# Attention and mixer block on one core: another order of operations, and twenty small operations on another engine

## The chip, the cores and the metric

The kernel runs on one core of one Trainium2 chip. The metric is the device time of one execution in microseconds (us); three executions of the kernel before gave 193.62, 194.53 and 194.60, so the median is 194.53. The five engines of a core are called PE (matmul), ACT (ScalarE), DVE (VectorE), POOL (GpSimd) and SP (SyncE, which here only issues transfers). Each runs its own instructions in order and waits for the others by semaphores.

## What is computed

x has 2048 rows of 448 numbers in bf16. Part A is an attention over 16 heads of 28 numbers in which each row sees 8 rows, itself and every second one before it; part B is a mixer that shifts quarters of the columns by one or two rows, followed by an MLP of width 1792.

```python
def _A_ref(x, wqkv, wo):
    W, dil = 8, 2
    ...
    logits = jnp.einsum("bhsd,bhswd->bhsw", q, kg) * scale
    attn = _softmax(logits, axis=-1)
    o = jnp.einsum("bhsw,bhswd->bhsd", attn, vg)
    return (...)(o, 0, 2, 1, 3).reshape(B, S, D) @ wo

def _B_ref(x, w1, w2, w3, w4):
    h = _gelu(_layernorm(x, axis=-1) @ w1)
    ...
    hs = jnp.concatenate([g0, g1, g2, g3], axis=-1) @ w2
    x1 = x + hs
    h2 = _gelu(_layernorm(x1, axis=-1) @ w3) @ w4
    return x1 + h2

h = x + _A_ref(_layernorm(x, axis=-1), A_wqkv, A_wo)
h2 = h + _B_ref(_layernorm(h, axis=-1), B_w1, B_w2, B_w3, B_w4)
```

## The kernel before

**Tiling and stages.** The 2048 rows are 16 tiles of 128, in four blocks t = 0 to 3 of 512 rows. All weights and x lie in SBUF once loaded. Part A runs for each block through N1 (layernorm, line 663), A1 (queries and keys, 679), V (values, 720), A2 (741) and A3 (788); part B through B1 (834), B2 (873), W3 (911) and B3 (928). The stages of part B behind B1 use other groups of tiles, the units u = 0 to 4 with tiles 0-1, 2-5, 6-9, 10-13 and 14-15.

The names that the prediction uses, each with its block or unit as a digit:
- A2: VectorE multiplies queries with shifted keys into `qk_r` (128 x 4096, three times a block, and once 128 x 2048), PE sums over `zc`. S: softmax on VectorE and ScalarE; its last product, into `pb`, is on VectorE or, by a table, on GpSimd; PE transposes `pb` and the result is copied out of PSUM.
- A3: VectorE spreads the weights over a mask into `bd_r`, PE multiplies by `vw` (the values, shifted by transfers from `vt` into `vw`; a few such transfers a block), and the results are copied into `actT`. O: the output projection with `wo_s`, added to x in `xin`.
- B1: layernorm of block t (its last step, the norms, writes `lntm`); a DMA transpose of 128 x 2048 numbers turns `lntm` into `actT`; M: PE multiplies by w1 (`w_s` in the profile's names), ScalarE applies gelu and writes into `arena`.
- B2: PE multiplies by w2 (`ps<-w_s,arena`), VectorE adds into `arena`; T: layernorm of unit u and its DMA transpose into `actT` (half as wide for units 0 and 4). W3: PE multiplies by w3, ScalarE's gelu writes `h3T`. B3: PE multiplies `h3T` by w4, VectorE adds and writes `ost`, which SyncE stores.

M0, W30, T0 and so on are these stages for block or unit 0. Where a sum of PE is made of two halves of 64 partitions, two groups run in pairs (`duo`).

**What sets the order.** The phases are recorded as 891 numbered operations, and one table, `ORDER` (lines 19 to 50), is a permutation of these numbers. `arrange` (192) goes through it: the operations of each engine are issued in the order of the table, each waiting by semaphores only for what it reads, overwrites or needs a buffer of. A second table, `OTHER` (51 to 53), names operations that take their alternative engine: a copy out of PSUM (`copy`, 397) or a norm (`normalize`, 552) goes to VectorE instead of ScalarE, and the product into `pb` (776) to GpSimd instead of VectorE. All instructions are issued at line 994, except the loads of ScalarE's table for exponentials and logarithms (989), so lines do not tell the groups of the profile apart; their tile names do.

All transfers go out on SyncE's queue, in the order of the table. For DMA transposes one rule is added: a transpose waits until the one before it and all plain transfers between the two have landed, and a plain transfer waits until the transposes before it have landed. Stores of results (their channel is callable) are exempt.

```python
if op.insts[0][0] == "dma_start_transpose":
    op.deps.update(turned + moved)
    turned, moved = [op], []
elif op.is_dma and not callable(op.chan):
    op.deps.update(turned)
    moved.append(op)
```

w1 and w2 are loaded by eleven transfers, w3 and w4 by two halves each (896 and 784 KB; `arena<-in_B_w_dram` in the profile).

Of the kernel before, what the change touches and what calls it, by code (L numbers as in the profile page):

```python
# [16 lines left out]
POWER = {'N1': 'aaaa', 'B1': 'aaaa', 'B2': 'apapp'}  # L17
RESIDUAL = 'ttvv'
ORDER = """
# [30 lines left out]
"""  # L50
OTHER = """
104 127 196 197 199 402 408 411 519 525 528 582 583
"""
FULL = (4,)
FILL = (1, 1, 0, 0)
# [980 lines left out]
```

## Time and profile before

| what | value |
|---|---|
| median of three executions | 194.53 us |
| span of the profiled execution, first to last instruction | 192.0 us |
| DMA traffic | 17.04 MB, 89 GB/s over the span |
| chain that ended last | PE 67%, DMA 13%, ACT 12%, DVE 3%, SyncE's queue 2% |
| DMA transposes | 9, of 4.4 us (median from issue to landing) |

The profiled execution's own time is its span; the executions that were timed lie some 2.5 us above it. Rows of the profile read: start in us, duration in us, engine, line, operation, tile written <- tiles read, shape and type, xcount for several merged, and in brackets the idle time of the engine ahead of it with what ended it. "PE ... 64*128 64x512" is a matmul of 64 rows of weights by 128 columns with 512 columns of data. `SPq` is SyncE's queue; its rows last as long as the issuing, not the transfer. Rows of a table by stages begin with the stretch from:to and then give the busy time of the engines.

### The profile page before, as it was taken

The page shows a single profiled execution, that of the slowest core. Times are in us where ns is not written, and L with a number is a line of the kernel's source. Part 1 is how long each engine was busy: PE and PEld are TensorE (multiplying, and loading weights), DVE is VectorE, ACT ScalarE, POOL GpSimd, SP SyncE. Part 2 cuts the span into 40 slices and gives each one's busy share as a digit, 9 for nine tenths or more (in the row PEclk, how much of TensorE's full clock was granted, in tenths as well). Part 3 has the DMA queues.
Part 4 walks back from the last instruction along what each step waited for, and adds up shares of the span by engine and source line. Part 5 has one row for each costly group of instructions (what it writes and reads, how often), then busy time and mean ns, then how long its engine had stood idle before and what let it go on. Part 6 is the DMA issues. An engine that isn't in the chain of part 4 may idle for free.

```text
span 192.0 us, 5741 instructions
## 1 busy us (share of the span) xinstructions
PE 181.2 (94%) x2482; PEld 92.6 (48%) x2482; DVE 129.6 (67%) x229; ACT 133.0 (69%) x310; POOL 29.3 (15%) x63
## 2 busy tenths in 40 slices
PE   6999999999999869969999999999999999999994
PEld 2584533453444333337545444455444544555672
DVE  7899999999999999999876970036988022002203
ACT  4489999999999999998595898860158004731340
POOL 3240000000004000201067000022077700000000
DMA  5998792005504163935905014006200542000111
GB/s 146 353 282 175 194 295 44 14 0 133 133 3 90 23 66 72 319 64 125 113 3 106 8 34 103 0 0 126 58 26 1 109 106 73 0 3 0 51 48 48
DMA packets 30273, 17.04 MB, mean 89 GB/s; under 512 B 18936, under 2 KB 29736, under 8 KB 30248
## 3 DMA queue, kind: packets, MB, share of 16 engines
q1 hardware_dynamic: 30248, 16.68, 37.1%
q8 instruction: 19, 0.31, 0.7%
q14 instruction: 6, 0.05, 0.1%
HBM read 8.04 MB, written 1.84 MB: 51 GB/s over the span
## 4 chain that ended last, share of the span: by engine, by line
PE 67%; DMA 13%; ACT 12%; DVE 3%; SPq 2%; issue 1%; POOL 0%; POOLq 0%; ACTq 0%
PE ps L994 67%; DMA actT<-lntm 7%; DMA arena<-in_B_w_dram 3%; ACT lntm L994 3%; ACT arena L994 3%; DMA vw<-vt 2%; ACT vt L994 2%; SPq L994 2%; DVE bd_r L994 2%; ACT h3T L994 1%; ACT actT L994 1%; ACT xin L994 1%; DVE lntm L994 1%; DVE ost L994 1%; ACT ls L994 1%
## 5 line engine op out<-in xcount | busy, mean ns | idle before, releaser
L994 PE MATMUL ps<-actT,arena 64*128 64x256 bf16 (+1 forms) x756 | 68.7, 329 | 2.2 <-DMA actT<-lntm 1.7
L994 ACT ACTIVATE h3T<-ps 128x512 bf16<-128x512 f32 (+1 forms) x70 | 30.3, 525 | 40.1 <-PE ps L994 40.0
L994 PEld LDWEIGHTS ps<-actT,arena 64*128 64x128 bf16 x756 | 35.4, 94 | 31.6 <-DMA actT<-lntm 2.1
L994 PE MATMUL ps<-arena,h3T 64*128 64x448 bf16 (+2 forms) x434 | 44.4, 343 | 0.0
L994 ACT ACTIVATE arena<-ps 128x512 bf16<-128x512 f32 (+10 forms) x86 | 40.1, 515 | 3.3 <-PE ps L994 2.5
L994 DVE SCALAR_TENSOR_TENSOR ost<-ps,mrs,arena 128x448 bf16<-128x448 f32 (+1 forms) x17 | 10.7, 652 | 36.5 <-PE ps L994 36.5
L994 DVE TENSOR_TENSOR qk_r<-arena 128x4096 bf16<-128x4096 bf16 (+1 forms) x16 | 32.0, 2016 | 0.4 <-ACT arena L994 0.2
L994 PEld LDWEIGHTS ps<-arena,h3T 64*128 64x128 bf16 (+1 forms) x434 | 23.0, 94 | 18.7 <-issue 0.2
L994 POOL TENSOR_TENSOR arena<-arena,xin 128x448 f32<-128x448 f32 x16 | 17.2, 1088 | 45.0 <-DVE lntm L994 45.0
L994 DVE TENSOR_TENSOR bd_r<-arena,bmask 80x2048 bf16<-80x2048 bf16 x16 | 19.0, 1216 | 1.6 <-PE ps L994 0.9
L994 ACT ACTIVATE actT<-ps 128x512 bf16<-128x512 f32 (+2 forms) x21 | 14.6, 742 | 2.1 <-PE ps L994 2.1
L994 PE MATMUL ps<-actT,w_s 64*128 64x512 bf16 x112 | 13.3, 377 | 1.7 <-DMA actT<-lntm 1.2
L994 PE MATMUL ps<-wo_s,actT 64*128 64x448 bf16 x128 | 14.3, 350 | 0.1
L994 PE MATMUL ps<-arena,actT 64*128 64x448 bf16 x112 | 12.4, 350 | 0.4 <-ACT vt L994 0.4
L994 PE MATMUL ps<-w_s,arena 64*128 64x448 bf16 x112 | 11.6, 350 | 1.0 <-ACT arena L994 0.9
L994 ACT ACTIVATE lntm<-xin,nm 128x448 bf16<-128x448 bf16 x16 | 10.5, 660 | 2.6 <-DVE nm L994 2.6
L994 DVE SCALAR_TENSOR_TENSOR arena<-xin,rs_y,ps 128x448 f32<-128x448 bf16 x16 | 10.3, 672 | 2.2 <-PE ps L994 2.2
L994 DVE TENSOR_SCALAR lntm<-arena,mv,rs_y 128x512 bf16<-128x512 f32 x14 | 10.2, 773 | 2.1 <-POOL rs_y L994 2.0
L994 POOL TENSOR_TENSOR pb<-ls,mx 128x512 bf16<-128x512 f32 x2 | 3.3, 1641 | 52.8 <-ACT mx L994 52.8
L994 DVE BATCH_NORM_STATS2 st<-xin 128x6 f32<-128x448 bf16 x16 | 9.4, 614 | 0.8 <-DMA xin<-in_A_x_dram 0.7
L994 PEld LDWEIGHTS ps<-actT,w_s 64*128 64x128 bf16 x112 | 5.1, 94 | 8.9 <-PE ps L994 1.7
L994 PEld LDWEIGHTS ps<-wo_s,actT 64*128 64x128 bf16 x128 | 5.6, 94 | 6.7 <-PE ps L994 1.4
(73 smaller groups left out, 161.7 us busy)
## 6 DMA issues: line engine op xcount, KB each, us to landing
arena<-in_B_w_dram SPq DMA_DIRECT2D x2, 896.0 KB, 7.3
out_dram<-ost SPq DMA_DIRECT2D x15, 112.0 KB, 1.9
arena<-in_B_w_dram SPq DMA_DIRECT2D x2, 784.0 KB, 5.7
vw<-vt SPq DMA_DIRECT2D x4, 320.0 KB, 4.3
vw<-vt SPq DMA_DIRECT2D x4, 256.0 KB, 4.2
arena<-in_A_wqkv_dram SPq DMA_DIRECT2D x2, 448.0 KB, 4.6
xin<-in_A_x_dram SPq DMA_DIRECT2D x2, 448.0 KB, 7.5
xin<-in_A_x_dram SPq DMA_DIRECT2D x3, 224.0 KB, 5.6
```

The source lines that it names most:

```text
L994: inst = getattr(eng, meth)(**kw)
```

## The change

The table `ORDER` is written anew, so that the operations of every engine are issued in another order, and `OTHER` names other operations. Nothing else differs: the same 891 operations, tiles and buffers. Of `OTHER`'s entries, thirteen operations go from ScalarE to VectorE (98, 106, 414, 417 and 534, copies into `actT`; 129, 134, 253 and 365, copies of keys and their edges; 256, into `vt`; 404 and 522, softmax results; 198, a norm of block 0), seven from VectorE to ScalarE (104, 127, 408, 411, 525, 528; 196, another norm of block 0), and one, 161, the product into `pb` of S0, from VectorE to GpSimd. ScalarE so has 266 operations instead of 272, VectorE 224 instead of 219, GpSimd 60 instead of 59. ScalarE's instructions whose first partition differs from that of the one before are 50 instead of 36.

```diff
 ORDER = """
-43 8 7 2 11 0 1 49 44 45 6 9 10 12 5 39 13 40 42 58 59 60 61 63 64 62 70 68 50 51 52 53 54 55 56 57 14 65 66 71 69 67
...
+43 0 1 7 39 2 40 41 8 58 59 60 11 9 63 5 64 61 62 10 68 65 66 70 69 71 67 72 73 74 75 78 46 44 49 50 51 52 53 54 55 56
...
 """
 OTHER = """
-104 127 196 197 199 402 408 411 519 525 528 582 583
+98 106 129 134 161 197 198 199 253 256 365 402 404 414 417 519 522 534 582 583
 """
```

SyncE's queue before, first from w2's last pieces through w3's two halves, then from block 0's transpose on (DMA_TRANSPOSE of 128x16x128 are those of blocks 0 to 3 and units 1 to 3, of 128x8x128 those of units 0 and 4; the pieces of w4 are 128x7x448):

```order
L994 DMA w2_s<-in_B_w2_dram 48x448
L994 DMA w2_s<-in_B_w2_dram 64x448 x2
L994 DMA vw<-vt 64x4x512
L994 DMA arena<-in_B_w3_dram 128x2x1792
L994 DMA vw<-vt 16x3x512
L994 DMA arena<-in_B_w3_dram 128x2x1792
L994 DMA vw<-vt 16x512
```

```order
L994 DMA_TRANSPOSE actT<-lntm 128x16x128 x2
L994 DMA vw<-vt 16x3x512
L994 DMA arena<-in_B_w4_dram 128x7x448
L994 DMA vw<-vt 16x512
L994 DMA arena<-in_B_w4_dram 128x7x448
L994 DMA_TRANSPOSE actT<-lntm 128x8x128
L994 DMA vw<-vt 80x4x512
L994 DMA vw<-vt 64x4x512
L994 DMA_TRANSPOSE actT<-lntm 128x16x128 x3
```

And the same part of the queue now, where w2's last pieces and w3 come behind the copies of block 2 into `vw`:

```order
L994 DMA w2_s<-in_B_w2_dram 64x448 x2
L994 DMA arena<-in_B_w3_dram 128x2x1792
L994 DMA_TRANSPOSE actT<-lntm 128x16x128
L994 DMA arena<-in_B_w3_dram 128x2x1792
L994 DMA_TRANSPOSE actT<-lntm 128x16x128
L994 DMA_TRANSPOSE actT<-lntm 128x8x128
L994 DMA arena<-in_B_w4_dram 128x7x448
L994 DMA vw<-vt 64x4x512
L994 DMA vw<-vt 16x3x512
L994 DMA arena<-in_B_w4_dram 128x7x448
L994 DMA vw<-vt 80x4x512
L994 DMA_TRANSPOSE actT<-lntm 128x16x128
```

Unit 0's transpose has moved ahead of w4, right behind that of block 1, and w3's second half stands between the transposes of blocks 0 and 1. The loads of w1 and w2, which stood ahead of all copies into `vw`, now stand among those of blocks 1 and 2: w1 behind the first copy of block 2 and w2 behind two more.

PE before, from M1 (by w1) through block 1's part of B2 (by w2) and W30 (`ps<-actT,arena` of 256 columns) to B30:

```order
L994 MATMUL ps<-actT,w1_s 128x512 x28
L994 MATMUL ps<-qk_r,zc 32x32x8x2 x8
L994 MATMUL ps<-wo_s,actT 128x448 x8
L994 MATMUL ps<-qk_r,zc 32x32x8x2 x8
L994 MATMUL ps<-wo_s,actT 128x448 x8
L994 MATMUL ps<-qk_r,zc 32x32x8x2 x4
L994 MATMUL ps<-w2_s,arena 128x448 x28
L994 MATMUL ps<-actT,arena 128x256 x56
L994 MATMUL ps<-ident,pb 80x64 x16
L994 MATMUL ps<-actT,arena 128x256 x42
L994 MATMUL ps<-arena,h3T 128x448 x28
L994 MATMUL ps<-bd_r,vw 32x64 x96
```

PE now, from the output projections of block 2 ahead of M1 on:

```order
L994 MATMUL ps<-wo_s,actT 128x448 x24
L994 MATMUL ps<-actT,w1_s 128x512 x14
L994 MATMUL ps<-wo_s,actT 128x448 x8
L994 MATMUL ps<-actT,w1_s 128x512 x8
L994 MATMUL ps<-qk_r,zc 32x32x8x2 x8
L994 MATMUL ps<-actT,w1_s 128x512 x6
L994 MATMUL ps<-actT,arena 128x256 x42
L994 MATMUL ps<-qk_r,zc 32x32x8x2 x12
L994 MATMUL ps<-w2_s,arena 128x448 x14
L994 MATMUL ps<-actT,arena 128x256 x8
L994 MATMUL ps<-w2_s,arena 128x448 x8
L994 MATMUL ps<-actT,arena 128x256 x6
```

W30 has moved ahead of the 28 matmuls by w2, with part of which it now alternates, and 24 instead of 16 projection matmuls stand between M0 and M1.

VectorE before, around unit 0's norms (`lntm<-arena,nm,rs_y`):

```order
L994 TENSOR_TENSOR qk_r<-arena 128x4096
L994 CAST actT<-ps 128x512
L994 TENSOR_TENSOR nmr<-nm,rs_y 128x2
L994 SCALAR_TENSOR_TENSOR xin,mv<-ps,xin 128x448 x2
L994 TENSOR_TENSOR qk_r<-arena 128x2048
L994 TENSOR_SCALAR lntm<-arena,nm,rs_y 128x512 x2
L994 SCALAR_TENSOR_TENSOR xin,mv<-ps,xin 128x448 x2
```

And now:

```order
L994 TENSOR_TENSOR qk_r<-arena 128x4096
L994 TENSOR_TENSOR nmr<-nm,rs_y 128x2
L994 TENSOR_SCALAR lntm<-arena,nm,rs_y 128x512 x2
L994 SCALAR_TENSOR_TENSOR xin,mv<-ps,xin 128x448 x4
L994 TENSOR_SCALAR nm<-mv 128x4
L994 TENSOR_TENSOR qk_r<-arena 128x4096
L994 TENSOR_TENSOR qk_r<-arena 128x2048
```

The four sums into `xin`, the `qk_r` product of half width and one of full width now stand behind the norms.

58 rows, old and new, of the table ORDER are left out of this document.

## The prediction

> **What bounds the kernel now.** I read the page's busy shares first, then the busy time by stages (engines in us of each stretch), then TensorE's rows in time where a stage is not full, and last the chain of waits over those places.
>
> ```profile
> PE 181.2 (94%) x2482; PEld 92.6 (48%) x2482; DVE 129.6 (67%) x229; ACT 133.0 (69%) x310; POOL 29.3 (15%) x63
> 50.00:60.00 10.00, 9.91 (x220) 4.61 (x218) 9.94 (x15) 9.97 (x28) 0.01 (x1) 1.00 0.10 29
> 60.00:70.00 10.00, 7.56 (x174) 3.54 (x170) 9.79 (x18) 9.79 (x21) 2.19 (x1) 1.00 0.28 54
> 70.00:80.00 10.00, 9.40 (x120) 3.67 (x122) 9.84 (x17) 9.78 (x22) 0.03 (x1) 1.00 0.83 169
> 80.00:90.00 10.00, 7.98 (x118) 4.58 (x112) 9.44 (x24) 9.15 (x25) 2.53 (x4) 1.00 0.55 141
> 90.00:100.00 10.00, 9.57 (x226) 5.62 (x226) 7.47 (x11) 7.84 (x18) 2.23 (x4) 1.00 0.46 56
> 100.00:140.00 40.00, 40.00 (x402) 19.31 (x400) 22.05 (x54) 25.07 (x48) 7.19 (x8) 1.00 0.25 52
> ```
>
> The columns after the stretch are PE, PEld, DVE, ACT, POOL, the granted clock (1.00 everywhere), the DMA share and GB/s. PE is 94% busy, yet what can be won is all in one place: from 60 to 100 us PE lacks 2.44 + 0.60 + 2.02 + 0.43 = 5.49 us, and in the same stretch until 90 us VectorE and ScalarE are 92 to 98% busy. From 100 us on PE is full (40.00 of 40.00). So the end is the start of the last gap-free run of PE, plus the work behind it.
>
> ```profile
> 63.60 3.67 PE L994 MATMUL ps<-actT,w_s 64*128 64x512 bf16 x28 [0.77 <-DMA actT<-lntm]
> 74.18 3.43 PE L994 MATMUL ps<-actT,w_s 64*128 64x512 bf16 x28 [0.33 <-ACT rs_x L994]
> 85.71 3.47 PE L994 MATMUL ps<-actT,arena 64*128 64x256 bf16 x56 [1.66 <-DMA actT<-lntm]
> 96.07 1.25 PE L994 MATMUL ps<-actT,w_s 64*128 64x512 bf16 x10 [0.43 <-DMA actT<-lntm]
> ```
>
> These are M0, M1, W30 and M2: each begins when a DMA transpose has landed. The chain of waits tells why those land so late:
>
> ```profile
> 68.82 5.27 DMA actT<-lntm
> 76.09 6.49 DMA arena<-in_B_w_dram
> 82.60 3.06 DMA actT<-lntm
> 85.71 2.49 PE ps L994 x42
> 90.60 5.43 DMA actT<-lntm
> 96.07 92.72 PE ps L994 x981
> ```
>
> It is a row of transfers on SyncE's queue: block 1's transpose, w4's second half, T0's transpose, and at last block 2's transpose (90.60), with which the gap-free run of 92.72 us begins.
>
> **T0's transpose no longer waits for w4.** A transpose waits for all plain transfers queued since the one before (the rule of `arrange`), so T0's was issued at 82.60, when w4's second half had landed at 76.09 + 6.49 = 82.58, though its rows were ready earlier:
>
> ```profile
> 79.35 1.00 DVE L994 TENSOR_SCALAR lntm<-arena,nm,rs_y 128x512 bf16<-128x512 f32 x2
> 76.91 0.62 DVE L994 SCALAR_TENSOR_TENSOR xin<-ps,xin 128x448 bf16<-128x448 f32 x1
> 78.21 1.23 DVE L994 TENSOR_TENSOR qk_r<-arena 128x2048 bf16<-128x2048 bf16 x1
> 69.85 2.28 DVE L994 TENSOR_TENSOR qk_r<-arena 128x4096 bf16<-128x4096 bf16 x1
> ```
>
> The norms ended at 80.35, so 2.25 us were lost to w4. The new VectorE order also puts these norms ahead of two sums into xin (0.55 each by their starts), a half qk_r product (1.1) and a whole one (2.2), 4.4 us; of the operations that VectorE takes over (below) some 1.5 us stand ahead. That leaves 2.9 less, so they end near 77.5. With 3.06 of transfer the rows land at 80.6 instead of 85.67. PE gets there from M1's start (74.2 to 75.8, below) by 3.43, eight wo and eight zc matmuls (0.76 and 0.45 by starts), so at 78.9 to 80.5: W30's wait shrinks from 1.66 to between 0 and 1.7, five us earlier. Late next is VectorE.
>
> **Block 2's transpose then hangs on its norms alone.** Before, it was issued at 90.60, when copies queued behind T0's transpose had landed; its norms were done at 89.76 (89.38 + 0.38):
>
> ```profile
> 89.38 0.38 DVE L994 TENSOR_SCALAR lntm<-xin,nm,rs_y 128x512 bf16<-128x512 bf16 x1
> 85.68 1.38 SPq L994 DMA_DIRECT2D vw<-vt  x2
> ```
>
> The copies now follow a transpose that lands 5 us earlier; of w4's two halves among them the second goes out some 2 us behind that landing (three issues of 0.69, half of 1.38) and lands 6.49 later, at 89.1, just ahead of the norms. VectorE's work up to those norms is nearly that of before: what went behind T0's norms still stands ahead of these, two statistics of mixer rows and what goes with them (1.2 us) now stand behind, and the 1.5 us of added operations come on top: +0.3. VectorE lacks 0.56 us in 80 to 90 and was full before that, so the norms end at 89.4 to 90.3 and M2 starts at 94.9 to 95.8: I take 95.5, a gain of 0.5 (0.2 to 1.1). Ahead of M2 the new PE order also places one more pair of w4 groups and two fewer of attn·v:
>
> ```profile
> 104.02 1.49 PE L994 MATMUL ps<-arena,h3T 64*128 64x448 bf16 x14
> 94.65 0.99 PE L994 MATMUL ps<-bd_r,vw 80*32 80x64 bf16 x96
> ```
>
> That is 1.33 (to the next start) less 2 x 0.27, so 0.8 us of the 92.72 is done ahead of M2, in time that PE spent waiting. Behind M2 the order holds the same matmuls in other places; W32 now meets its transpose with little to spare, 0 to 0.5 there, and I take 0. **Sum:** 0.5 + 0.8 = 1.3 us less, between 0.4 and 1.9.
>
> **What speaks against: w3's second half between two transposes.** All weights of part B now come later in SyncE's queue, behind block 1's and partly block 2's copies into vw, and w3's halves stand around block 0's transpose.
>
> ```profile
> arena<-in_B_w_dram SPq DMA_DIRECT2D x2, 896.0 KB, 7.3
> arena<-in_B_w_dram SPq DMA_DIRECT2D x2, 784.0 KB, 5.7
> 44.94 3.22 SPq L994 DMA_DIRECT2D vw<-vt  x4
> 42.58 0.42 PE L994 MATMUL ps<-bd_r,vw 80*32 80x64 bf16 x32
> 59.07 11.62 SPq L994 DMA_TRANSPOSE actT<-lntm  x2
> 67.50 1.29 DVE lntm L994 x4
> ```
>
> Block 2's copies wait for PE's attn·v of block 0 (over at 43.0 before, some 1.3 us more work ahead of it now). Behind that, eight transfers at 0.81 (3.22 / 4) put w3's first half at 51, landing at 57 to 58.3, ahead of block 0's norms (issue at 59.07): nothing lost. If all fifteen queue from 43, it is 55 and 61 to 62. Block 0's transpose, issued at 59.07, let M0 start at 63.60; then the second half goes out and takes 5.7 to 7.3 (the near rows: smaller, or shared), so block 1's transpose goes at 69.2 to 70.8 instead of 68.82, where its norms ended. M1 starts 0.4 to 2.0 later, with eight wo matmuls (0.76) more ahead of it, so PE loses nothing to 1.2 there. T0's norms hang less on M1 than on B20, which this does not move; so I count it at nothing for the end, up to +1.2 in the range. By the Trainium skill, "DMA: Bandwidth & Descriptors", sections "Where 436 GB/s comes from" and "Latency and other measured facts", HBM gives a core about 358 GB/s and a transfer costs some 2 us besides. For 896 KB that makes an estimate of 4.6 us, and block 1's transpose would not be delayed at all; the rows here, 5.7 and 7.3, are slower, and I keep to them.
>
> **The engine moves.** Thirteen small operations go from ScalarE to VectorE, seven come the other way and one goes from VectorE to GpSimd: six fewer on ScalarE, five more on VectorE. Costed at 0.3 to 0.6 each by their starts, VectorE has 0.9 us more ahead of block 0's norms.
>
> ```profile
> 57.27 1.05 DVE L994 TENSOR_SCALAR lntm<-xin,nm,rs_y 128x512 bf16<-128x512 bf16 x3
> 58.23 0.81 ACT L994 ACTIVATE lntm<-xin,nmr,rs_y 128x512 bf16<-128x512 bf16 x1
> 61.19 1.43 ACT L994 ACTIVATE xin<-ps 128x448 bf16<-128x448 f32 x3
> 62.64 0.49 ACT L994 ACTIVATE arena<-ps 64x64 bf16<-64x64 f32 x2
> 54.70 0.60 ACT L994 ACTIVATE actT<-ps 128x512 bf16<-128x512 f32 x1
> 55.18 0.55 ACT L994 ACTIVATE vt<-ps 128x448 bf16<-128x448 f32 x1
> ```
>
> VectorE's three norms ended at 58.3 but ScalarE's fourth at 59.04, so 0.7 of the 0.9 is covered. ScalarE normally overlaps its neighbours by 0.12 (54.70 + 0.60 against 55.18); where the first partition changes, there is a gap of 0.02 (62.62 to 62.64). Counted over its instructions, such changes rise from 36 to 50: 14 x 0.14 = 2 us, which eats the 1.4 us or so that six fewer operations save up to block 0. Zero on balance; +0.9 if the cover goes.
>
> S0's product into pb (0.68 on VectorE) goes to GpSimd, beside a qk_r product:
>
> ```profile
> 59.99 2.21 POOL L994 TENSOR_TENSOR pb<-ls,mx 128x512 bf16<-128x512 f32 x1 [47.99 <-ACT mx L994]
> 86.13 1.07 POOL L994 TENSOR_TENSOR pb<-ls,mx 128x512 bf16<-128x512 f32 x1 [4.84 <-ACT mx L994]
> 58.98 2.28 DVE L994 TENSOR_TENSOR qk_r<-arena 128x4096 bf16<-128x4096 bf16 x1
> ```
>
> So 1.07 alone and 2.21 beside one: 0.4 to 1.5 later for the transposes that read it. PE reaches them with 2.6 us more work done than before, which hides that; without cover up to +1.5. By the Trainium skill, "SBUF — State Buffer", section "Who interferes with whom", whichever of the two starts second is fully blocked until the first ends. The rows agree (qk_r ended at 61.26, the product 0.94 later); in the worst case that would be 2.28 + 1.07 = 3.35 us, still with 2.6 of cover, which adds nothing to the sum.
>
> **Rivals.** *Weights too late (slower).* If w3's first half lands past 59.1 and its second past 70.8, each transpose of the queue goes later by what is missing: with the slow end above, M0 starts 2.2 late and M1 3 late. From W30 on the order gives back 1.3; 1.7 us more, 196.2. It decides once w3's first half is issued later than 52. For it: two engines full, one queue in order, a slow end worked out from rows. Against: eight transfers, not fifteen, stand behind the last wait.
> *VectorE and ScalarE carry more (slower).* They are full until 90 us; if the 0.9 and the pauses' 2 us pass on to block 2's norms undiminished, M2 starts 1.8 later less 0.8: 195.5. So the plan's own count of pauses may be right and the order worse for it.
> *Nothing moves (same).* M2 stays at 96 since VectorE sets it, and W32's wait eats the 0.8: 194.5.
> *All of it (faster by more).* The waits at W30 and M2 go (2.02 + 0.43) with half a microsecond at M0: 3.0 less, 191.5.
>
> **How the numbers follow.** The profiled span is 192.0, the median run 194.53, 2.5 above it; the sum is a difference and holds for both: 194.5 - 1.3 = 193.2, span 190.7. Chances: forecast 0.44, all of it 0.10, nothing moves 0.10, weights too late 0.22, fuller engines 0.14. About 1 us (0.5%) is what a measurement tells from no change. Of the forecast 0.36 is faster, 0.08 same (its own range is 192.6 to 194.1, with W32's wait); so faster 0.46, same 0.17, slower 0.37. The range 191.0 to 196.6 reaches into both sides' cases.
>
> **What would show it.** Right: T0's transpose issued before 78 with no w4 ahead of it, W30 starting near 80.6, M2 near 95.5 and PE without gaps behind it, 1.3 us of PE's 5.49 gone between 60 and 100. Wrong: M0 later than 64 or block 1's transpose issued past 71 with w3's second half as its releaser; block 2's norms later than 90.5; w4's second half landing past 90; or gaps of PE behind 100 us, where there were none.

## The result, and the profile after

Four executions of the changed kernel took 196.7 us in the median (195.84 to 197.11), four of the kernel before 194.34 (193.62 to 194.60): a ratio of 1.0125, interval 1.0094 to 1.0156. The change makes the kernel slower by 1.2%. The profiled execution has a span of 194.0 us instead of 192.0. Ratios, here and below, leave out executions more than 1.5% above the fastest of their kernel; the only profile below of such an execution is that of the run that moves T0's transpose alone.

The page's busy shares and the table by stages of the changed kernel (columns as before):

```profile
PE 183.0 (94%) x2482; PEld 93.1 (48%) x2482; DVE 131.0 (68%) x234; ACT 132.4 (68%) x304; POOL 30.2 (16%) x64
60.00:70.00 10.00, 8.08 (x176) 3.89 (x172) 10.00 (x18) 9.66 (x24) 1.86 (x2) 1.00 0.57 146
70.00:80.00 10.00, 9.04 (x100) 3.53 (x100) 8.88 (x18) 8.23 (x19) 1.03 (x1) 0.83 0.45 65
80.00:90.00 10.00, 9.39 (x130) 5.15 (x128) 8.44 (x14) 9.83 (x26) 0.22 (x1) 1.00 0.88 231
90.00:100.00 10.00, 9.35 (x146) 5.04 (x142) 9.29 (x19) 7.42 (x14) 2.52 (x3) 1.00 0.35 68
```

From 60 to 100 us PE now lacks 1.92 + 0.96 + 0.61 + 0.65 = 4.14 us instead of 5.49. That looks like the 1.3 us that the prediction wanted, and it isn't: from 70 to 80 us the granted clock is 0.83, so part of what counts as busy there is the same work done at a lower clock. A table of busy time can't be read without its clock column.

PE's rows in time, at the places of the prediction, with the last row of PE:

```profile
64.03 3.20 PE L994 MATMUL ps<-actT,w_s 64*128 64x512 bf16 x28
69.06 0.70 PE L994 MATMUL ps<-bd_r,vw 80*32 80x64 bf16 x64 [1.48 <-ACT arena L994]
70.76 2.67 PE L994 MATMUL ps<-w_s,arena 64*128 64x448 bf16 x14 [1.00 <-ACT arena L994]
81.48 1.05 PE L994 MATMUL ps<-actT,arena 64*128 64x256 bf16 x16
97.50 3.19 PE L994 MATMUL ps<-actT,w_s 64*128 64x512 bf16 x28 [0.34 <-DMA actT<-lntm]
108.77 3.41 PE L994 MATMUL ps<-actT,arena 64*128 64x512 bf16 x30
183.21 2.80 PE L994 MATMUL ps<-actT,arena 64*128 64x256 bf16 x48 [1.03 <-ACT h3T L994]
185.93 5.50 PE L994 MATMUL ps<-arena,h3T 128*128 128x448 bf16 x42
```

And the same last row of the kernel before:

```profile
183.94 5.50 PE L994 MATMUL ps<-arena,h3T 128*128 128x448 bf16 x42
```

M0 starts at 64.03 (63.60 before) and W30 at 81.48 (85.71), 0.9 us behind the 80.6 that was foretold. M2 starts at 97.50 instead of 96.07, and PE ends at 191.43 instead of 189.44. So the 2.0 us are 1.43 that M2 is late and 0.56 behind it, where less work is left than before (below). Behind M2 there are now places where PE stands: 0.05 us ahead of W31 (108.77, by the chain below) and 1.03 us ahead of W34 (183.21). The chain of waits shows what each start hung on:

```profile
78.30 3.05 DMA actT<-lntm
84.18 8.95 DMA vw<-vt
93.14 4.32 DMA actT<-lntm
97.50 11.22 PE ps L994 x198
108.77 73.43 PE ps L994 x750
183.21 8.25 PE ps L994 x90
```

T0's transpose goes out at 78.30, 0.8 us behind the prediction's 77.5. Block 2's (93.14) follows a copy into `vw` that took 8.95 us, and the gap-free run of PE of before is broken into three.

### The profile page after: what moved, and what is told of

Same layout as the page of the kernel before. It is cut to its first block, busy times and chain, and to the rows that moved or that the text cites. A ratio compares the mean times of both kernels' runs of the same rounds, so it can differ in the third digit from the quotient of the medians.

```text
span 194.0 us, 5747 instructions
## 1 busy us (share of the span) xinstructions
PE 183.0 (94%) x2482; PEld 93.1 (48%) x2482; DVE 131.0 (68%) x234; ACT 132.4 (68%) x304; POOL 30.2 (16%) x64
## 4 chain that ended last, share of the span: by engine, by line
PE 70%; DVE 10%; DMA 9%; ACT 6%; issue 2%; SPq 1%; ACTq 0%
PE ps L994 70%; DMA vw<-vt 5%; DVE qk_r L994 4%; DMA actT<-lntm 4%; ACT arena L994 2%; SPq L994 1%; DVE st L994 1%; ACT lntm L994 1%; DMA xin<-in_A_x_dram 1%; DVE lntm L994 1%; DVE arena L994 1%; ACT L994 1%; DVE nm L994 1%; DVE mx L994 1%; ACT xin L994 1%
## 5 line engine op out<-in xcount | busy, mean ns | idle before, releaser
L994 PE MATMUL ps<-actT,arena 64*128 64x512 bf16 (+1 forms) x756 | 69.9, 329 | 2.0 <-ACT h3T L994 1.0
L994 ACT ACTIVATE arena<-ps 128x512 bf16<-128x512 f32 (+8 forms) x83 | 39.9, 509 | 5.0 <-PE ps L994 4.0
L994 POOL TENSOR_TENSOR arena<-arena,xin 128x448 f32<-128x448 f32 x16 | 16.6, 1058 | 18.5 <-DVE lntm L994 18.5
L994 PE MATMUL ps<-w_s,arena 64*128 64x448 bf16 x112 | 13.5, 369 | 1.1 <-ACT arena L994 1.0
L994 DVE TENSOR_SCALAR lntm<-arena,mv,rs_y 128x512 bf16<-128x512 f32 x14 | 8.5, 667 | 7.0 <-ACT rs_y L994 4.5
L994 POOL TENSOR_TENSOR rs_y<-rs_x,mhalf 128x4 f32<-128x4 f32 (+1 forms) x3 | 3.6, 1193 | 34.9 <-DVE mv L994 27.4
```

Source lines behind the costliest of these rows:

```text
L994: inst = getattr(eng, meth)(**kw)
```

## The experiments

In the diffs the numbers are those of `ORDER`, one to a row. 37 and 38 are w4's halves, 586, 440 and 649 the transposes of T0, block 2 and T1, 685 and 827 the stores of tiles 3 and 11. Ratios are to the kernel before.

### The tail: one late store

VectorE's rows near the end of the changed kernel:

```profile
178.37 1.28 DVE L994 SCALAR_TENSOR_TENSOR ost<-ps,mrs,arena 128x448 bf16<-128x448 f32 x2 [16.30 <-PE ps L994]
182.38 1.27 DVE L994 SCALAR_TENSOR_TENSOR ost<-ps,mrs,arena 128x448 bf16<-128x448 f32 x2 [2.73 <-DMA out_dram<-ost]
```

`ost` has three buffers. Tile 3's sum is done 34 us earlier, but its store stands behind that of tile 11 in SyncE's queue, so one buffer is held, and the sum at 182.38 has to wait until another store has landed. Meanwhile PE stops at 183.21; its row names ScalarE's gelu as what it waited for, and that the store is behind it is what the next run is for.

```diff
 684
+685
 ...
 827
-685
```

> The changed kernel with one store moved: that of block of rows 384 to 511 is issued right behind the addition that writes it, instead of behind the stores of unit 3 at 183.5. Theory A (it holds one of three ost buffers until the end, so unit 3's third addition waits for the landing of a store at 182.28 and PE stands 1.03 us at 183.21 for the PSUM bank that this addition reads): that wait goes, 1.0 to 1.2 less, about 195.6. Rival B (the wait of W34 comes from ScalarE's gelus in their order): nothing changes, 196.7 and the wait stays.

Measured: 194.95 us, 1.0044 (1.0016 to 1.0071) where the change has 1.0125. PE passes W34 without a wait (in its profile this row begins earlier, with other matmuls merged):

```profile
182.11 3.98 PE L994 MATMUL ps<-actT,arena 64*128 64x256 bf16 x70
```

So the store is about two thirds of the loss (0.81 of 1.25%). The mirror of it on the kernel before:

```diff
 690
+691
 ...
-685
 ...
-691
 ...
 827
+685
```

> The kernel before with the store of one output tile (tile 3) moved behind that of tile 11 in SyncE's queue, as the change has it; so that a buffer is free in between, the store of tile 4, which stood late there, is put directly behind its sum. Theory A (a late store keeps one of three output buffers, and the sums of the tail then wait for another store's landing): PE waits 0.8 to 1.5 us near 181 us ahead of W34's matmuls, ratio 1.004 to 1.008. Rival B (the late store of tile 4 already did the same in the kernel before, or the tail has slack): no such wait, ratio 0.998 to 1.002.

0.9996 (0.9976 to 1.0016), no wait: a miss for theory A as it was put. In the old order of the tail the next sum is due only when PE has finished, long after the other two stores:

```profile
181.63 1.28 DVE L994 SCALAR_TENSOR_TENSOR ost<-ps,mrs,arena 128x448 bf16<-128x448 f32 x2 [4.22 <-PE ps L994]
```

So the store's late place cost something only together with an order that needs the third buffer soon.

### GpSimd's product

> The changed kernel with S0's product into pb back on VectorE, nothing else. Theory A (the product on GpSimd holds up VectorE: a 0.16 us operation on nm took 1.04 us beside it at 31.7, ScalarE then idled 1.04 and PE 1.07 at 36.6): those three waits go, and the time falls by 0.7 to 1.1, to about 195.8. Rival B (the 0.68 us that VectorE takes back costs as much as it saves, since VectorE is full until 70 us): within 0.3 of the changed kernel's 196.7.

The edit takes 161 out of `OTHER`. 196.72 us, 1.0136 (1.0097 to 1.0176): nothing gained. And the move alone in the kernel before:

```diff
-104 127 196 197 199 402 408 411 519 525 528 582 583
+104 127 161 196 197 199 402 408 411 519 525 528 582 583
```

> The kernel before with one engine move alone: S0's product into pb goes from VectorE to GpSimd. In the run with all twenty-one moves PE waited 0.92 us at 36.23, where the kernel before did not, and ended 3.6 us later. Theory A (this one move, by holding VectorE's small operation and ScalarE behind it, makes the first microsecond of that loss): PE waits 0.7 to 1.0 us more at 36, M0 starts 0.4 to 0.7 us later than 63.60, ratio 1.002 to 1.006. Rival B (it makes most of the loss, through all later stages): ratio 1.010 or more. Rival C (PE's cover hides it, as the prediction had it): ratio 0.998 to 1.002.

1.0011 (0.9977 to 1.0044): no cost that this can tell. In the changed kernel the rows at that place do show a stall,

```profile
31.35 1.38 POOL L994 TENSOR_TENSOR pb<-ls,mx 128x512 bf16<-128x512 f32 x1 [19.66 <-ACT mx L994]
31.72 1.04 DVE L994 TENSOR_SCALAR nm<-mv 128x4 f32<-128x4 f32 x1
```

an operation of 128x4, the like of which took 0.16 in the kernel before, and which here ends with GpSimd's product. A3's second group of matmuls on block 0 starts at 41.52 us without the move and at 41.51 with it. But ahead of the stall PE was 0.29 us later in the profile without the move (31.22 against 30.93 at the same matmuls), so about 0.3 us of the stall is left by then and the rest is made up for.

### Order alone, engine moves alone

> The old ORDER with the new OTHER: only the twenty-one operations change engine, every operation keeps its place in the table. Theory A (the order costs, the engines do not): the ratio to the kernel before is 0.997 to 1.003, M0 starts within 0.3 us of 63.60 and M2 within 0.3 us of 96.07. Rival B (the engines carry it: VectorE's 0.9 us more ahead of block 0's norms and ScalarE's 14 more pauses pass on to block 2's norms): the ratio is 1.005 to 1.010, and M2 starts 1 to 2 us later.

> The new ORDER with the old OTHER: every operation stays on the engine of the kernel before, the order is that of the change. Theory A (the two parts of the change are made for each other, and the order needs the moves as the moves need the order): 1.010 to 1.025. Rival B (the moves are the loss, 1.020 alone, and the order is a gain of about half a per cent): 0.990 to 1.000. Rival C (the order alone makes the loss of the change and the moves add nothing in it): 1.010 to 1.015, with M0 and M2 within 0.4 us of the changed kernel's 64.03 and 97.50; A and C are told apart by where M0 and M2 start, A has them later than 64.5 and 98.

The first has the old `ORDER` and the new `OTHER`, the second the reverse. Moves alone: 197.7 us, 1.0201 (1.0164 to 1.0238). Order alone: 199.73, 1.0233 (1.0160 to 1.0306), M2 at 102.00. Both together: 1.0125. In the first, PE's waits grow at many places; three of the rows:

```profile
36.23 0.83 PE L994 MATMUL ps<-qk_r,zc 128*32 128x512 bf16 x12 [0.76 <-DVE qk_r L994]
76.44 3.43 PE L994 MATMUL ps<-actT,w_s 64*128 64x512 bf16 x28 [1.61 <-DMA actT<-lntm]
105.37 2.44 PE L994 MATMUL ps<-wo_s,actT 64*128 64x448 bf16 x24 [1.66 <-ACT arena L994]
```

So neither theory of "the one or the other" holds: each part costs 2% beside the old version of the other, and inside the new order the moves are worth 1.1%.

### The weights in SyncE's queue

T0's transpose ahead of w4, in the kernel before, with its norms early:

```diff
 581
+582
+583
+586
 425
 ...
-583
-582
 ...
-586
```

> The kernel before with one part of the change: unit 0's transpose stands ahead of w4's two halves in SyncE's queue, and its norms ahead of two sums into xin and the half qk_r product on VectorE; PE's order stays, with W30 behind block 1's part of B2. Theory A (the prediction's first two steps hold by themselves and were lost to the other moves of PE): the transpose is issued by 79.5 instead of 82.60, W30 starts by 84.2 instead of 85.71, block 2's transpose hangs on its norms, M2 starts at 95.0 to 95.7 instead of 96.07, ratio 0.993 to 0.998. Rival B (what is put behind T0's norms on VectorE comes late for block 2's norms by as much): the norms end at 90.5 or later instead of 89.76, M2 starts at 96.0 or later, ratio 0.999 to 1.004.

0.9995 (0.9956 to 1.0034). The profiled execution took 197.28 us, those behind the ratio 193.35 to 194.69, so what comes late in the profile need not be in them. In the profile neither theory holds: the transpose went out at 77.95, W30 began at 84.02 without a wait, the norms of block 2 ended at the old 89.76, and M2 began at 98.02. The rows in time of SyncE's queue, VectorE and PE:

```profile
83.26 1.37 SPq L994 DMA_DIRECT2D vw<-vt  x2
89.38 0.38 DVE L994 TENSOR_SCALAR lntm<-xin,nm,rs_y 128x512 bf16<-128x512 bf16 x1
92.12 2.72 SPq L994 DMA_TRANSPOSE actT<-lntm  x1
98.02 1.37 PE L994 MATMUL ps<-actT,w_s 64*128 64x512 bf16 x10 [3.15 <-DMA actT<-lntm]
```

The DMA table of 80.5 to 92 us (KB of each, median us from issue to landing):

```profile
arena<-in_B_w_dram SPq DMA_DIRECT2D x2, 784.0 KB, 6.0
vw<-vt SPq DMA_DIRECT2D x1, 320.0 KB, 8.2
vw<-vt SPq DMA_DIRECT2D x1, 256.0 KB, 8.1
```

Between T0's transpose and block 2's the queue now holds w4 and the copies. They share the DMA engines, and the last to land is not w4's second half (89.63) but the copy behind it (92.06): block 2's norms, done at 89.76, wait 2.4 us for it. In this profile the wait was not removed, it was passed on. Behind PE's 3.15 us at M2 the granted clock is 0.95 from 90 to 100 us and 0.88 from 100 to 110.

All loads early, in the changed kernel and with the two other repairs (store, 161):

> The changed kernel with all loads of wo, w1 to w4 put on SyncE's queue at 21 us, behind block 0's last copy into vw, so that no load stands between the transposes. Theory A (block 2's transpose was issued at 93.14 because w4 and three copies took 9 us to land; its norms ended at 92.04): it is issued with the norms, M2 starts 0.8 to 1.1 earlier and so does the end, about 195.7. Rival B (the loads at 21 to 40 us slow the copies into vw of block 1 and 2 and PE waits for those): M0 later than 64.5 and 197 or more. Rival C (block 2's norms set M2, and they do not move): within 0.3 of 196.7.

> The three edits together on the changed kernel: S0's product on VectorE, the one store early, all weights loaded early. If the three costs are independent of each other, the gains add: 196.7 less 2.7 to 3.3, about 193.7. If the early microsecond (theory A of the first) only moves the wait to a later transpose, 194.6. Rival: the order itself, without these three, is as slow as before the edits, 196 or more.

1.0159 (1.0113 to 1.0204) and 1.0054 (1.0026 to 1.0082): no gain from the loads. At block 2 they do what they were to do. In the first, whose profile has the full clock, VectorE's norms and SyncE's queue are:

```profile
90.17 1.37 DVE L994 TENSOR_SCALAR lntm<-xin,nm,rs_y 128x512 bf16<-128x512 bf16 x4
91.64 2.85 SPq L994 DMA_TRANSPOSE actT<-lntm  x1
```

The transpose goes out with the norms, 26.6 us behind M0 (65.01). In the run with 161 back on VectorE, also at full clock but with the weights in their new places, it goes out 28.1 us behind M0 (92.19 and 64.06), 1.4 us behind its norms, when a copy into `vw` has landed. But the early loads make M0 about 1 us later, and what is gained at M2 (96.46) is waited away ahead of W31 (0.88 us) and at the tail (1.50). In the second run, in which the clock falls as in the changed kernel, M2 begins at 97.48, no sooner than there. So the weights' places do hold block 2's transpose in the changed kernel, and taking the weights away in this way is worth nothing at the end.

w4 directly behind w3 in the kernel before (`37` and `38` behind `36`), without and with T0 early:

> The kernel before with w4's two halves loaded directly behind w3's second half, long before the transposes; nothing else moves. In the kernel before and in every kernel of the change w4 and three copies into vw share the queue near block 2's transpose, and that lands late. Theory A (w4's place in the queue is the wait that the prediction saw; it has to go ahead of all, not behind T0): T0's transpose is issued at 80.4 with its norms, W30 starts near 84.0 instead of 85.71, block 2's transpose is issued at 89.8 to 90.0 with its norms, M2 starts at 94.5 to 95.2, ratio 0.992 to 0.996. Rival B (the early load delays the copies of blocks 0 and 1, or what is gained is waited away at W31): M0 later than 64, or a new wait of PE near 105 to 109; ratio 0.998 to 1.004.

> The kernel before with w4 early and T0's norms and transpose early as well (both single edits together). Theory A (as for w4 alone; T0's early norms add at most 0.3, since W30 waits for block 1's part of B2 on PE anyhow): W30 at 84.0, M2 at 94.5 to 95.2, ratio 0.991 to 0.996. Rival B (T0's norms ahead of the sums into xin make block 2's norms later): norms end past 90.2, M2 at 95.5 or later, ratio 0.997 or more.

1.0077 (1.0034 to 1.0120) and 1.0078 (1.0038 to 1.0118), slower: so early they meet the copies of blocks 0 and 1, and in the first PE waits at 36 us for ScalarE's values, which had waited 1.52 us for a copy into `vw`:

```profile
36.12 0.93 PE L994 MATMUL ps<-arena,actT 64*128 64x448 bf16 x8 [1.99 <-ACT vt L994]
```

With M0 at 66.38 and 67.71 these two tell little about M2. The queue has a gap, from 48 us to block 0's transpose at 59; w4 in it, without T0's move and with it:

```diff
 386
+37
+38
 ...
-37
 ...
-38
```

> The kernel before with w4's two halves directly behind block 2's last copy into vw (issue near 48 us), where SyncE's queue has nothing until block 0's transpose at 59.07; in the run with w4 behind w3 they met the copies of blocks 0 and 1 and PE waited 2.1 us at 36. Theory A (w4 and the copies that wait with it are what holds T0's and block 2's transposes): both halves land by 58, M0 stays at 63.6 within 0.3, T0's transpose is issued at 80.4, block 2's at 89.8 to 90.0 with its norms, M2 starts at 94.6 to 95.2 instead of 96.07, ratio 0.992 to 0.997. Rival B (the end does not follow M2: a gain there is waited away by W31 or later): M2 the same, but PE waits anew near 105 to 109 and the ratio is 0.998 to 1.002.

> The same and T0's norms and transpose early, as the change has them. Theory A (T0 early is worth nothing by itself, since W30 waits for block 1's part of B2 on PE): as with w4 alone, ratio within 0.002 of it. Rival B (T0 early is worth its 1.7 us once nothing is queued behind it): M2 at 94.5 or earlier and a ratio lower by 0.003 or more.

0.9982 (0.9952 to 1.0013) and 0.9978 (0.9946 to 1.0009): at most a little. In the second, with its norms ending at 89.86, block 2's transpose goes out with them, and M2 begins where the prediction had it:

```profile
89.47 0.39 DVE L994 TENSOR_SCALAR lntm<-xin,nm,rs_y 128x512 bf16<-128x512 bf16 x1
95.26 2.98 PE L994 MATMUL ps<-actT,w_s 64*128 64x512 bf16 x26 [0.28 <-DMA actT<-lntm]
```

The two copies that took 8.2 and 8.1 us beside w4 take half as long here (DMA table of 81 to 87 us):

```profile
vw<-vt SPq DMA_DIRECT2D x1, 320.0 KB, 4.3
vw<-vt SPq DMA_DIRECT2D x1, 256.0 KB, 4.2
```

So the rows show why block 2's transpose was late with w4 behind T0. What that costs in time they do not show: the ratios with T0 early, 0.9995 with w4 behind it and 0.9978 with w4 in the gap, cannot be told apart.

And with the norms ahead of five statistics of mixer rows (634, 626, 629, 635 and 630 behind 438):

> The kernel before with w4 in the gap of the queue, T0 early, and on VectorE block 2's four norms ahead of five statistics of mixer rows. Theory A (with no weight in its way block 2's transpose hangs on VectorE's norms, and M2 on that transpose until PE is full): the norms end near 88.3 instead of 89.86, M2 starts 0.3 to 0.5 us sooner, when PE gets there, ratio 0.994 to 0.997. Rival B (T1's statistics, now later, hold W31, or the end does not follow): ratio 0.998 to 1.002.

193.37 us, 0.9962 (0.9929 to 0.9994): faster than both kernels, if only just. M2 has no wait left:

```profile
87.08 1.65 DVE L994 TENSOR_SCALAR lntm<-xin,nm,rs_y 128x512 bf16<-128x512 bf16 x4
95.22 2.98 PE L994 MATMUL ps<-actT,w_s 64*128 64x512 bf16 x26
```

### T1's rows at W31

In the changed kernel T1's statistics (three `mv`, `rs_x`) stand behind two `bd_r` products. With the early store, and these ahead (4 sets a constant on GpSimd that 640 needs):

```diff
 529
+4
+626
+630
+638
+627
+639
+640
```

> The changed kernel with the early store of the run before (the output tile of tile 3 stored directly behind its sum), and T1's statistics put ahead of two bd_r products on VectorE. Theory A (T1's rows are the gate at W31, and eat what is gained ahead of it): T1's transpose is issued 0.7 to 1.1 us sooner against M2's start, PE's wait of about 0.5 us ahead of W31 goes, and the ratio falls from 1.0044 to 1.000 to 1.003. Rival B (M2's late start alone sets W31; T1 only looks late): no wait goes that does not come back behind it, ratio 1.003 to 1.007.

1.0069 (1.0041 to 1.0097): no gain, the wait is still there, 0.64 us in its profile. The same with the weights out of the way (w1 to w3 behind block 0's last copy into `vw`, as in the run with all loads early, w4 in the gap), without and with T1's statistics early:

> The changed kernel with the early store, with w1, w2 and w3 loaded where the kernel before loads them (behind the copies of block 0) and w4 behind block 2's last copy. In it no weight stands between or behind transposes. Theory A (the weights' new places hold M2 in the changed kernel, and the earlier try lost it again at M0 by collisions): M0 by 64.0, block 2's transpose is issued with its norms near 91.5, M2 by 96.6, the same matmuls 0.8 us further than in the kernel before: ratio 0.996 to 1.001. Rival B (T1's rows near 108.8 are the gate whenever M2 starts): PE waits 0.8 us or more ahead of W31, ratio 1.002 to 1.006.

> The same and T1's statistics ahead of two bd_r products. Theory A (with M2 early, T1's rows are next): the wait ahead of W31 shrinks by 0.5 to 1.0 us against the kernel without this edit, the ratio falls by 0.002 to 0.005. Rival B (T1's statistics are not what holds its rows): no difference beyond 0.0015.

1.0107 (1.0070 to 1.0145) and 1.0044 (1.0017 to 1.0071). This is not the place that the kernel before has for w1 to w3: there they stand ahead of block 0's copies and among them, the last issued at 21.94 us, in the second of these runs at 31.58. That place was not tried. M0 is late in both (65.75 and 64.65). The second is no better than the early store alone, though no weight is near and block 2's transpose goes out with its norms (92.49): W31 still waits, and T1's transpose, issued at 103.35, took 6.1 us. PE's row:

```profile
109.52 2.76 PE L994 MATMUL ps<-actT,arena 64*128 64x512 bf16 x24 [0.79 <-DMA actT<-lntm]
```

The DMA table of 103 to 110 us, and that of 107.4 to 108.4:

```profile
actT<-lntm SPq DMA_TRANSPOSE x1, 6.1
```

```profile
DMA packets 6, 0.02 MB, mean 17 GB/s; under 512 B 5, under 2 KB 5, under 8 KB 5
q8 instruction: 1, 0.02, 5.8%
q1 hardware_dynamic: 5, 0.00, 0.6%
```

For a whole microsecond there is one packet of 16 KB of the kind "instruction", and five small ones of the transpose, of which the last go out behind it. The test: T1's last two norms ahead of a copy into `actT`, so that the transpose would be through before that packet (the edit of the store and of T1's statistics, and `534` behind `644`).

> The changed kernel with the early store, T1's statistics ahead of two bd_r products, and T1's last two norms ahead of a copy into actT. In the changed kernel's variants T1's transpose takes 4.9 to 6.1 us where transposes without a packet of 16384 bytes of the instruction kind among theirs take 4.25 to 4.40; that packet goes out near 107.2, just when the transpose's last packets are due. Theory A (that packet is part of the gate at W31): issued 0.7 us sooner, near 102.6, the transpose is through before the packet, lands by 107.2, PE's wait ahead of W31 goes and the ratio is 0.999 to 1.003. Rival B (the transpose's length has another cause): it takes 5 us or more again, the wait stays at 0.3 us or more, ratio 1.003 to 1.007.

194.47 us, 1.0012 (0.9977 to 1.0046). The transpose went out at 100.81, partly since this profile had the full clock, took 4.3 us, and W31's wait is gone. Its DMA table from 100.5 to 108.5, its chain from M2 on, and PE's last row:

```profile
actT<-lntm SPq DMA_TRANSPOSE x1, 4.3
```

```profile
96.40 92.53 PE ps L994 x1038
```

```profile
183.41 5.51 PE L994 MATMUL ps<-arena,h3T 128*128 128x448 bf16 x42
```

The profiled execution took 193.31 us. The run does not settle whether the packet held W31. The packet went out sooner as well, at 104.71, and again 3.9 us behind the transpose's issue, as in the run with T1's statistics early (there 103.31 and 107.23); it only just missed the transpose's last packet, at 104.60. And issued at 100.81 the rows would have landed by 106.8 even in the 6.0 us of that run, ahead of PE, which came to W31 at 107.46. So T1's earlier issue is enough to end the wait.

The edits at two places, both behind M2's start in what they free, so take the change from 1.2% slower to no difference that can be told. The last step alone, from 1.0069 to 1.0012, has intervals that just overlap.

## Why the prediction was wrong

It said 193.2 us, faster; measured were 196.7, just past the upper end of its range. By its sum PE was to end 1.3 us sooner, at 188.1; it ended at 191.4. Of these 3.3 us 2.0 lie at M2's start and 1.3 behind it. (The chances of its cases add up to 0.18 for the same time and 0.36 for slower, not 0.17 and 0.37.) Step by step:

**T0's transpose early: right, and no gain alone.** Norms near 77.5, rows at 80.6 were said; issue at 78.30, rows at 81.35, W30 at 81.48 (77.39, 80.46 and 80.60 in the run with 161 on VectorE, at full clock). In the run with only this move W30 could not use it, since block 1's part of B2 stands ahead on PE until 84. With w4 in the gap the ratio is 0.9982 without this move and 0.9978 with it.

**"Block 2's transpose then hangs on its norms alone", M2 at 95.5: the step that failed.** The transpose was to go out with norms that end at 89.4 to 90.3. It went out at 93.14, and M2 came at 97.50. Both halves of the step were off, the norms by about 2.2 us against the middle of that range and the copies by 1.1 more; the transpose itself took 4.32 us instead of 5.43, which gave 1.1 back.

The copies: the working let w4's second half land at 89.1 and left out the copy behind it in the queue, though the rule of `arrange` makes the transpose wait for it as well. It took w4's half at the 6.49 us of before, where one copy went with it; with three of them in the same stretch it took 9.08 and landed at 92.33, and the copy behind it took 8.95 and landed at 93.12. The runs show the same copies at half that time once w4 stands in the gap, and there the forecast's 95.5 comes true (95.26, in the order before). By the Trainium skill, "DMA: Bandwidth & Descriptors", section "Latency and other measured facts", a transfer has some 2 us of its own and the bytes on top. w3's first half, nearly alone in the queue, agrees: issued at 52.74, it took 4.85 us against the estimate of 4.6. The same estimate for w4's second half, of fewer bytes, would be below 4.6, against the 9.08 that it took beside the copies.

The norms ended not at 89.4 to 90.3 but at 92.05. Their rows, in the changed kernel and then in the run with 161 on VectorE, whose profile has the full clock from 70 to 80 us:

```profile
90.67 1.38 DVE L994 TENSOR_SCALAR lntm<-xin,nm,rs_y 128x512 bf16<-128x512 bf16 x4
```

```profile
89.38 1.38 DVE L994 TENSOR_SCALAR lntm<-xin,nm,rs_y 128x512 bf16<-128x512 bf16 x4
```

In the last variant, also at full clock, they end at 90.8. So about 1.2 of some 2 us go with the clock, which the prediction took as 1.00 everywhere; what remains would be the new PE order, in which W30 stands ahead of the last `zc` sums of block 3 and of B2, so that VectorE gets its input later. That part was not tried by itself, and its cause stays open.

**0.8 us of PE's work pulled ahead: right.** From M2 to PE's end it was 93.37 us before (189.44 - 96.07); in the variant without gaps it is 92.52 (188.92 - 96.40), 0.85 less.

**"Behind M2 the same matmuls in other places", no waits: wrong.** From M2 to the end the changed kernel took 93.93, 1.4 more than the gap-free variant: 1.03 at the tail, the rest in small pieces (ahead of W31 only 0.05 in this profile, but 0.65 in that of the run with 161 on VectorE). The prediction looked at W32 and not at the stores, whose place in the queue the new table moved too, nor at VectorE's order ahead of T1's norms. Most of the loss lies in these two: with both repaired the kernel is level with the kernel before, though M2 is as late as ever where the clock falls (97.47 in the run with T1's statistics early) and 0.3 late where it doesn't (96.40). What M2's 1.43 us cost by themselves is an estimate: less the 0.85 pulled ahead, some 0.6.

**w3's second half between two transposes, costed 0: right.** Block 1's transpose was issued at 70.29, as its norms ended; w3's half had landed at 70.10. It was no more than 0.2 us from costing something. w3's first half was issued past the rival's limit of 52, at 52.74, and still landed at 57.59, ahead of block 0's norms, since it took 4.85 us and not 6 to 7.3. The rival "weights too late" came nearest in time (196.2) but by another mechanism: M0 was at 64.03, and the delay sat at block 2. Of the signs named for being wrong, four came: block 2's norms past 90.5, w4's second half past 90 (it landed at 92.33), waits of PE behind 100 us, and M0 past 64, by 0.03.

**Engine moves, 0 on balance: wrong as a term.** The sum treated moves and order as parts that add. Alone, the order costs 2.3% and the moves 2.0%, and together 1.2%: counting pauses and saved operations gave neither. The rival "VectorE and ScalarE carry more" had the norms late and M2 1.8 us later (how 2.9 us of work become 1.8 is not worked out there); with the moves alone M2 is at 97.98, 1.91 later. But inside the new order the moves are worth 1.1%, so the norms' lateness in the changed kernel is not shown to come from them.

**GpSimd's product, hidden: right in effect.** The cover held but for some 0.3 us at block 0, which the ratios do not show, though what was blocked was not only GpSimd. By the Trainium skill, "SBUF — State Buffer", section "Who interferes with whom", the one that comes second is fully blocked. The rows agree: VectorE's 0.16 us became 1.04. The prediction had thought of the product as the one that waits, and never of a tiny operation behind it with ScalarE in its train.

## What to carry to other kernels

When a transfer is moved past another in one queue, ask who now stands behind it and add up everything that shares the engines until the next wait, not the largest piece alone. Check an order where it has no slack, also at its end: which buffer is held by a store that is late, and what is due when it is needed. Do not cost an order and an assignment of engines as a sum: here each alone cost more than both together.

## What the runs showed of the hardware

**T1's transpose took longer where an instruction packet went out ahead of its last packet.** The page counts 19 packets of queue 8, kind "instruction", 16 KB each, 0.9 to 1.8 us long.

```profile
q8 instruction: 19, 0.31, 0.7%
```

In twenty profiles (all runs told of here, with before and after) T1's transpose takes 4.9 to 6.1 us in the eight where such a packet goes out 0.8 us or more before the transpose's last one, and 4.3 to 4.6 in the twelve where it goes out with that last one or later. The store that the tail waits for (issued 179.08) took 3.2 us with such a packet going out from 179.82 to 181.05; the same store in the kernel before, 1.8 us, with the packet 1.5 us behind its issue. These are observations in profiles. The one run that was to separate the two did not: the transpose's length went from 6.0 to 4.3 us, but the packet moved with it and missed its last packet by 0.11 us.

**The clock can fall after a few short waits.** Two waits of 1.48 and 1.00 us between 67.5 and 70.8 us were followed by a granted clock of 0.83 from 70 to 80 in the changed kernel, and the fourteen matmuls by w2 took 2.67 us; in the profile of the last variant, with nearly the same waits, the clock was 1.00 and they took 1.74 (its table by stages, then PE's row):

```profile
70.00:80.00 10.00, 8.99 (x114) 3.45 (x114) 9.89 (x23) 9.59 (x21) 1.03 (x1) 1.00 0.47 81
```

```profile
70.81 1.74 PE L994 MATMUL ps<-w_s,arena 64*128 64x448 bf16 x14 [1.00 <-ACT arena L994]
```

So the same order can meet it or not. The Trainium skill, "TensorE: Matmul & The Clock Gate", section "What's actually happening", has half the clock after an idle window of some 3.4 us that runs on by itself; 0.17 of 10 us at half the clock is an estimate of 3.4 us, which agrees. No wait here is as long as the window; the clock fell after two short ones. What a fall goes with in time shows in the last variant's twelve executions: four with a mean granted clock of 0.999 or 1.000 took 192.96 to 194.07 us, five with 0.991 194.19 to 194.72, and three with 0.982 195.53 to 195.75. The change's loss is not explained by it: of the changed kernel's four executions the one with 1.000 took 196.79 us, the three with 0.991 195.84 to 197.11.
